# Two row blocks of a gMLP input normalized and transposed earlier, in the seam between two stages

## The chip, the cores and the metric

The kernel runs on one core of a Trainium2 chip. The metric is the device time of one execution in microseconds (us), the median of several runs. Unless another source is named, times inside the execution come from one profiled execution and are counted from the start of its span.

## The reference, cut to what matters

A transformer-like block in bf16: a recurrent attention with a small memory, then a gated MLP that also mixes over the sequence (gMLP). B is 1, S is 2048, the model width 512.

```python
h  = x + A(layernorm(x))          # A: 64 segments of 32 rows, 32 heads of 128, each segment
                                  #    attends to itself and to 8 memory rows that the segment before left
xn = layernorm(h)
z  = gelu(xn @ w_in)              # 512 -> 2 x 896
z1 = z[:, :896]
z2 = layernorm(z[:, 896:])
g  = w_sp @ z2 + b_sp[:, None]    # mixes over the 2048 rows
h2 = h + (z1 * g) @ w_out
```

`layernorm` has no scale and no offset here.

## The kernel before, in words

Everything lies in one function, `fast_path`. It writes out the instructions of every engine by hand, in program order: a small emitter appends each instruction to its engine's list, finds its dependences by named tokens, and turns them into semaphore waits. So the order in the text is the order of every engine's queue. There is no planner. (A general path for inputs that would overflow stands behind a flag and does not run.)

**Rows and row blocks.** The 2048 rows are 16 row blocks of 128 (`RB` is 16, blocks 0 to 15). `h` of a block is held in `hbuf`, two slots, block parity choosing the slot.

**First stage.** A loop over the 64 segments does the attention. Every fourth segment a block of `h` is finished by `h_done` (L691 to L697): an add on DVE (VectorE, L666), the two instructions of the layernorm's statistics on DVE (L691, L692), `1/sqrt` on POOL (GpSimd, L693 and L695), and a store of `h`. `xn2_apply` (L700, DVE) then normalizes the block into `xo`, two slots. For blocks 0 to 13 that is done inside the loop, and the block is stored to DRAM and fetched back transposed by a DMA. `z2_narrow` (L735) already computes the pre-activations of the second half of `z` for blocks 0 to 9 inside the loop, and parks them in DRAM; `z2_back` (L888) loads them again. Block 14's `h_done` is the last thing in the loop, block 15's comes after it.

**Second stage, the loop around the change (L1137 and on).** Blocks 10 to 15 are its six steps, `k` from 0 to 5:

- `z2_mm` (L1060, PE = TensorE, 8 matmuls of 128x448) and its two gelus on ACT (ScalarE, L1063) give the second half of `z` for block 10 + k.
- `z1_some(4)` (L1092, 16 matmuls of 128x512, and four gelus on ACT, L1095) does four of the 28 groups of the first half of `z`. A group covers four row blocks at once, so it needs their transposed `xn`.
- `z2_gelu` (L1123, ACT, 128x896) activates two of the parked blocks, 2k and 2k + 1.
- `z2_norm` (L1074 twice, L1076, DVE, then L1078 and L1080 on POOL) takes the layernorm statistics of a `z2` block, `z2_apply` (L1085, DVE) applies them a step later.
- `mix0` (L1099, PE, 5 matmuls of 128x512 for a `z2` block) starts the mixing over rows for five of the seven feature blocks of the first 512 columns, with the blocks that were normalized in the step before. It starts in the third step, with 15 matmuls.

In step 0, the work left over from the first stage comes between: `F_group` (L661) and `WoX_mm` (L676) on PE, four groups of `z1_some`, `WoX_scatter` (L686), then `h_done(15)`.

**Blocks 14 and 15** are not sent through DRAM. They are transposed by PE (L1159, four instructions of 128x128 for a block, from `xo` into a PSUM bank) and copied out by DVE: `xn_copy` (L1055). In the kernel before, `xn2_apply` of block 14 stands in step 1 and of block 15 in step 2; the transposes and copies of block 14 stand in step 2 and of block 15 in step 3. `z2_mm` of block 14 comes in step 4, of block 15 in step 5.

**PSUM banks.** `zbank()` hands out banks 5, 6 and 7 in turn: to each half of `z2_mm`, to each group of `z1_some` and to the transposes of a block. Each of them therefore waits until the one three takings before it has been read out, by ACT for a matmul group, by DVE's `xn_copy` for a transpose:

```python
zcnt = [0]

def zbank():
    zcnt[0] += 1
    return 5 + zcnt[0] % 3
```

**After the loop**, the last four groups of `z1`, the rest of the mixing, the gating and the output matmuls follow, bounded by PE.

**DMA loads in the seam**, all issued from the queue of SP (SyncE) in this order: `w_in1`, transposed blocks 11 to 13, parked `z2`, `wT` for the first 512 columns (L884, eight pieces of 256 KB, read by `mix0`), the transposed blocks 8, 9 and 10 (L714), the bias, `wT` for the second 512 columns, `w_out`, and `h` again.

Of the kernel before, what the change touches and what calls it, by code (L numbers as in the profile page):

```python
# [169 lines left out]
def fast_path(nc, st, keep, A_x, A_mem0, A_Wq, A_Wk, A_Wv, A_Wo, A_seg_len, B_w_in, B_w_sp, B_b_sp, B_w_out, out):  # L170
# [8 lines left out]
    RB = S // 128  # L179
    DC = D // 128  # L180
# [17 lines left out]
    def sb(name, shape, dt):  # L198
        return st.enter_context(nc.sbuf_tensor("f_" + name, shape, dt))
# [32 lines left out]
    xo = sb("xo", [128, 2, 512], BF)  # L232
    wst = sb("wst", [128, RB, 64], BF)
    ident = sb("ident", [128, 128], BF)
# [26 lines left out]
    psb = ps.bitcast(BF)  # L261
# [4 lines left out]
    def PB(b):  # L266
        return ("ps", b)

    def sp(fn, **k):
        return em.add("sp", fn, dma=True, **k)  # L270

    def pe(fn, **k):
        return em.add("pe", fn, **k)
# [4 lines left out]
    def dve(fn, **k):  # L278
        return em.add("dve", fn, **k)
# [378 lines left out]
    def F_group(rb, bank, stop=False):  # L658
        for j in range(4):
            i = (4 * rb + j) % 8  # L660
            pe(lambda e, i=i, j=j: e.matmul(ps[32 * j:32 * j + 32, bank, :], lhsT=F_sb[:, :], rhs=part[:, i, :], start=True, stop=stop,  # L661
                                            tile_position=(0, 32 * j)),
               reads=[("part", i, 0), ("part", i, 1), "F"], writes=[PB(bank)])
# [8 lines left out]
    def WoX_mm(rb, qr):  # L672
        for bg in range(8):
            b, g = bg // 4, bg % 4
            h = 16 * b + 4 * qr + g
            pe(lambda e, h=h, g=g, i=8 * qr + bg: e.matmul(ps[32 * g:32 * g + 32, WXB, :], lhsT=cTx[:, rb % 2, i, :], rhs=w_o[:, h, :],  # L676
                                                           start=(i < 4), stop=(i >= H - 4), tile_position=(0, 32 * g)),
               reads=[("cTx", rb % 2), ("Wo", h // 8)], writes=[PB(WXB)])

    def WoX_evac(rb):  # L680
        act(lambda e: e.activation(out=partx[:], in_=ps[:, WXB, :], func=ACT.Copy), reads=[PB(WXB)], writes=["partx"])

    def WoX_scatter(rb, bank, start=False):
        for c in range(4):
            q = slice(32 * c, 32 * c + 32)
            pe(lambda e, q=q, c=c: e.matmul(ps[q, bank, :], lhsT=Sc[:, q], rhs=partx[:], start=start, stop=True, tile_position=(0, 32 * c)),  # L686
               reads=["partx", "Sc"], writes=[PB(bank)])

    def h_done(rb, bank):
        F_add(rb, bank)  # L690
        dve(lambda e: e.bn_stats(out=stats[:, rb % 2, :], in_=hbuf[:, rb % 2, :]), reads=[("h", rb % 2)], writes=[("st", rb % 2)])  # L691
        dve(lambda e: e.bn_aggr(out=mv[:, rb, :], in_=stats[:, rb % 2, :]), reads=[("st", rb % 2)], writes=[("mv", rb)])  # L692
        pool(lambda e: e.tensor_scalar(out=rstd[:, rb:rb + 1], in0=mv[:, rb, 1:2], scalar1=EPS, scalar2=None, op0=ALU.add),  # L693
             reads=[("mv", rb)], writes=[("rstd", rb)])
        pool(lambda e: e.tensor_tensor(out=rstd[:, rb:rb + 1], in0=rstd[:, rb:rb + 1], in1=mhalf[:, 0:1], op=ALU.pow),  # L695
             reads=[("rstd", rb), "mhalf"], writes=[("rstd", rb)])
        sp(lambda e: e.dma_start(h_d[rb], hbuf[:, rb % 2, :]), reads=[("h", rb % 2)], writes=[("hd", rb)])  # L697

    def xn2_apply(rb, j):
        dve(lambda e: e.tensor_scalar(out=xo[:, j, :], in0=hbuf[:, rb % 2, :], scalar1=mv[:, rb, 0:1], scalar2=rstd[:, rb:rb + 1],  # L700
                                      op0=ALU.subtract, op1=ALU.mult),
            reads=[("h", rb % 2), ("mv", rb), ("rstd", rb)], writes=[("xo", j)])
# [17 lines left out]
    def xT2(rb):  # L720
        return xts[rb // 8][:, rb % 8, :, :]
# [160 lines left out]
    def load_wT(tb, after):  # L882
        for t in range(8):
            sp(lambda e, t=t: e.dma_start(wTb[tb % 2][:, t, :, :], wT_d[8 * tb + t]), reads=[("wTd", 8 * tb + t)],  # L884
               writes=[("wT", tb % 2, t)], after=after)
# [10 lines left out]
    for s in range(NSEG):  # L896
        j4 = s % 4
        rb = s // 4
# [154 lines left out]
    def xn_copy(rb, j, bank):  # L1053
        src = psb[:, bank, 0:512].rearrange("p (dc c) -> p dc c", dc=DC)
        dve(lambda e: e.tensor_copy(out=xT2(rb), in_=src), reads=[PB(bank)], writes=[("xn2T", rb)], after=[lastop["s"], lastop["x"]])  # L1055

    def z2_mm(rb, hf, bank):
        t, tok = xT2z(rb)
        for dc in range(DC):
            pe(lambda e, dc=dc: e.matmul(ps[:, bank, 0:HF], lhsT=t[:, dc, :], rhs=w_in2[:, dc, hf * HF:(hf + 1) * HF],  # L1060
                                         start=(dc == 0), stop=(dc == DC - 1)),
               reads=["w_in2", tok], writes=[PB(bank)])
        act(lambda e: e.activation(out=z2[:, rb, hf * HF:(hf + 1) * HF], in_=ps[:, bank, 0:HF], func=ACT.Gelu_apprx_tanh),  # L1063
            reads=[PB(bank)], writes=[("z2", rb, hf)], after=[lastV])
# [18 lines left out]
    def z2_apply(rb):  # L1083
        j = nslot[rb]
        dve(lambda e: e.tensor_scalar(out=z2[:, rb, :], in0=z2[:, rb, :], scalar1=mv2[:, j, 0:1], scalar2=rs2[:, j:j + 1],  # L1085
                                      op0=ALU.subtract, op1=ALU.mult),
            reads=[("z2", rb, 0), ("z2", rb, 1), ("mv2", j), ("rs2", j)], writes=[("z2", rb, 0), ("z2", rb, 1)])

    def z1_group(tb, fb, bank):
        r0 = 4 * tb  # L1090
        for dc in range(DC):
            pe(lambda e, dc=dc: e.matmul(ps[:, bank, 0:TB], lhsT=w_in1[:, dc, fb * 128:(fb + 1) * 128],  # L1092
                                         rhs=xts[r0 // 8][:, r0 % 8:r0 % 8 + 4, dc, :], start=(dc == 0), stop=(dc == DC - 1)),
               reads=["w_in1"] + [("xn2T", r) for r in range(r0, r0 + 4)], writes=[PB(bank)])
        act(lambda e: e.activation(out=z1T[:, fb, tb * TB:(tb + 1) * TB], in_=ps[:, bank, 0:TB], func=ACT.Gelu_apprx_tanh),  # L1095
            reads=[PB(bank)], writes=[("z1T", fb, tb)], after=[lastK])
# [15 lines left out]
# [3 lines that stand above are left out]
# [7 lines left out]
    def z2_gelu(rb):  # L1122
        act(lambda e: e.activation(out=z2[:, rb, :], in_=z2[:, rb, :], func=ACT.Gelu_apprx_tanh),  # L1123
            reads=[("z2", rb, 0), ("z2", rb, 1)], writes=[("z2", rb, 0), ("z2", rb, 1)])
# [6 lines left out]
    def z1_some(n):  # L1131
        for _ in range(n):
            if z1list:
                tb, fb = z1list.pop(0)
                z1_group(tb, fb, zbank())

    for k, rb in enumerate(range(NP, RB)):  # L1137
        z2_mm(rb, 0, zbank())
        if k == 0:
            F_group(RB - 1, XB)  # L1140
        z2_mm(rb, 1, zbank())
        if k == 0:
            for qr in range(4):
                WoX_mm(RB - 1, qr)
            endA = em.by_eng["pe"][-1]
            WoX_evac(RB - 1)
            load_wT(1, [endA])
            sp(lambda e: e.dma_start(w_out, B_w_out.rearrange("(fb p) d -> p fb d", p=128)), writes=["w_out"], after=[endA])
            z1_some(4)
            WoX_scatter(RB - 1, XB)  # L1150
            h_done(RB - 1, XB)
            for r in range(RB):
                sp(lambda e, r=r: e.dma_start(h_sb[:, r, :], h_d[r]), reads=[("hd", r)], writes=[("hs", r)], after=[lastQ])
        if k in (1, 2):
            xn2_apply(RB - 3 + k, k % 2)
        if k in (2, 3):
            r, j, bank = RB - 4 + k, (k - 1) % 2, zbank()
            for dc in range(DC):
                pe(lambda e, dc=dc, j=j, bank=bank: e.transpose(out=psb[:, bank, dc * 128:(dc + 1) * 128], in_=xo[:, j, dc * 128:(dc + 1) * 128],  # L1159
                                                                identity=ident[:, :]), reads=[("xo", j), "ident"], writes=[PB(bank)])  # L1160
            xn_copy(r, j, bank)
        for r in range(max(0, 2 * k - 2), min(NP, 2 * k)):
            z2_apply(r)
            mixq.append((k, r))
        z2_norm(rb)
        if k > 0:
            z2_apply(rb - 1)
            mixq.append((k, rb - 1))
            z1_some(4)
        for r in range(2 * k, min(NP, 2 * k + 2)):  # L1170
            z2_gelu(r)
            z2_norm(r)
        while mixq and mixq[0][0] < k:
            mix0(mixq.pop(0)[1])
# [28 lines left out]
    for tb in range(NTB):  # L1203
        for fb in range(len(ACC) if tb == 0 else 0, FB):
            if tb == 0:
                bank = 5 + fb % 3
            else:
                bank = gcnt % 2
# [785 lines left out]
```

## Time and profile before

| | |
|---|---|
| median of 3 runs | 886.18 us (884.33 to 886.44) |
| the profiled execution | 887.59 us, of which the span in the profile is 885.8 us |
| PE busy | 858.6 us, 97% of the span |
| DVE, ACT, POOL busy | 487.6, 457.3 and 110.6 us |
| mean granted TensorE clock | 0.994 |

The span runs from the first to the last instruction; 1.79 us of the profiled execution lie around it. PE is the TensorE matmul row, and "idle before" in a row is followed by the instruction that ended the idle time. The granted clock is a share of full speed. The loop described above lies between about 717 and 773 us.

### The profile page before, as it was taken

The page shows a single profiled execution, that of the slowest core. Times are in us where ns is not written, and L with a number is a line of the kernel's source. Part 1 is how long each engine was busy: PE and PEld are TensorE (multiplying, and loading weights), DVE is VectorE, ACT ScalarE, POOL GpSimd, SP SyncE. Part 2 cuts the span into 40 slices and gives each one's busy share as a digit, 9 for nine tenths or more (in the row PEclk, how much of TensorE's full clock was granted, in tenths as well). Part 3 has the DMA queues.
Part 4 walks back from the last instruction along what each step waited for, and adds up shares of the span by engine and source line. Part 5 has one row for each costly group of instructions (what it writes and reads, how often), then busy time and mean ns, then how long its engine had stood idle before and what let it go on. Part 6 is the DMA issues. An engine that isn't in the chain of part 4 may idle for free.

```text
span 885.8 us, 46595 instructions
## 1 busy us (share of the span) xinstructions
PE 858.6 (97%) x21446; PEld 488.5 (55%) x21453; DVE 487.6 (55%) x1128; ACT 457.3 (52%) x1147; POOL 110.6 (12%) x280
## 2 busy tenths in 40 slices
PE   6889999999999999999999999999999998999997
PEld 6645555565566655656565555555555543444443
DVE  3445556565556556565655565556555557364343
ACT  2346565666665656666665666466665575400000
POOL 1420111111111111010101011111101013200000
PEclk9999999999999999999999999999999999999999
DMA  9962232123320311211312121523222299032101
GB/s 320 377 177 63 64 57 61 44 59 63 60 58 25 84 46 32 65 45 52 60 43 52 46 66 47 102 69 78 73 62 67 62 244 333 2 101 76 62 13 38
DMA packets 109210, 76.35 MB, mean 86 GB/s; under 512 B 64104, under 2 KB 94512, under 8 KB 109008
## 3 DMA queue, kind: packets, MB, share of 16 engines
q1 hardware_dynamic: 108496, 73.04, 30.1%
q8 instruction: 170, 2.79, 1.3%
q14 instruction: 32, 0.26, 0.1%
q0 software_dynamic: 192, 0.20, 0.1%
q10 hardware_dynamic: 320, 0.07, 0.0%
HBM read 41.75 MB, written 20.91 MB: 71 GB/s over the span
## 4 chain that ended last, share of the span: by engine, by line
PE 94%; DVE 2%; issue 1%; DMA 1%; POOL 1%; ACT 0%; DVEq 0%
PE f_ps L481 26%; PE f_ps L625 13%; PE f_ps L575 12%; PE f_ps L1099 11%; PE f_ps L411 7%; PE f_ps L676 4%; PE f_ps L592 3%; PE f_ps L430 3%; PE f_ps L1188 3%; PE f_ps L1092 2%; PE f_ps L735 2%; PE f_ps L520 2%; PE f_ps L541 1%; PE f_ps L511 1%; PE f_ps L649 1%
## 5 line engine op out<-in xcount | busy, mean ns | idle before, releaser
L481 PE MATMUL f_ps<-f_arena,f_hT 128*32 128x512 bf16 x4096 | 240.3, 380 | 0.5 <-issue 0.2
L488 ACT ACTIVATE f_Tst<-f_ps 128x512 bf16<-128x512 f32 x256 | 145.9, 596 | 78.1 <-PE f_ps L481 77.9
L481 PEld LDWEIGHTS f_ps<-f_arena,f_hT 128*32 128x32 bf16 x4096 | 92.9, 96 | 104.0 <-ACT f_hT L654 32.7
L575 PE MATMUL f_ps<-f_arena,f_hT 128*32 128x512 bf16 x2048 | 140.4, 378 | 0.0
L625 PE MATMUL f_ps<-f_arena,f_cT 128*32 128x256 bf16 x4096 | 129.2, 274 | 0.9 <-ACT f_cT L611 0.8
L625 PEld LDWEIGHTS f_ps<-f_arena,f_cT 128*32 128x32 bf16 x4096 | 101.2, 97 | 21.7 <-ACT f_cT L611 18.7
L494 DVE STREAM_TRANSPOSE f_QT<-f_Tst 128x256 uint32<-128x256 uint32 x128 | 57.0, 446 | 91.7 <-ACT f_Tst L488 91.7
L1099 PE MATMUL f_ps<-f_arena 128*128 128x512 bf16 x448 | 100.9, 382 | 0.0
L613 DVE TENSOR_SCALAR f_cT<-f_ps 128x320 bf16<-128x320 f32 x128 | 56.9, 487 | 41.2 <-PE f_ps L598 41.2
L1099 PEld LDWEIGHTS f_ps<-f_arena 128*128 128x128 bf16 x448 | 44.1, 99 | 53.9 <-issue 2.2
L497 DVE STREAM_TRANSPOSE f_KT<-f_Tst 128x256 uint32<-128x256 uint32 x128 | 57.0, 445 | 29.1 <-ACT f_Tst L488 26.4
L411 PE MATMUL f_ps<-f_hTe,f_arena 128*128 128x128 bf16 x1024 | 68.0, 225 | 4.0 <-DVE f_arena L422 2.9
L611 ACT ACTIVATE f_cT<-f_ps 128x320 bf16<-128x320 f32 x128 | 49.0, 435 | 38.4 <-PE f_ps L598 38.4
L411 PEld LDWEIGHTS f_ps<-f_hTe,f_arena 128*128 128x128 bf16 x1024 | 60.3, 101 | 14.1 <-issue 9.5
L504 POOL COPY f_QT<-f_arena 128x256 bf16<-128x256 bf16 x64 | 30.7, 479 | 298.2 <-PE f_ps L526 298.1
L561 DVE SCALAR_TENSOR_TENSOR f_E_sb<-f_R_sb,f_E_sb 128x160 bf16<-128x160 f32 x128 | 41.7, 325 | 46.2 <-ACT f_R_sb L557 46.2
L642 DVE CAST f_part<-f_ps 128x256 bf16<-128x256 f32 x64 | 27.2, 425 | 68.9 <-PE f_ps L625 68.9
L553 ACT ACTIVATE f_R_sb<-f_ps 128x160 f32<-128x160 f32 x128 | 39.0, 305 | 37.9 <-PE f_ps L546 37.9
L575 PEld LDWEIGHTS f_ps<-f_arena,f_hT 128*32 128x32 bf16 x2048 | 45.2, 95 | 21.1
L1105 DVE TENSOR_TENSOR f_arena<-f_ps,f_arena 128x512 f32<-128x512 f32 x28 | 19.3, 690 | 60.7 <-PE f_ps L1099 60.7
L654 ACT ACTIVATE f_hT<-f_ps 128x16 bf16<-128x16 f32 x126 | 23.2, 184 | 55.1 <-PE f_ps L649 54.7
L633 POOL COPY f_cTx<-f_cT 128x256 bf16<-128x256 bf16 x64 | 25.6, 400 | 197.1 <-DVE f_cT L613 197.1
(113 smaller groups left out, 1165.8 us busy)
## 6 DMA issues: line engine op xcount, KB each, us to landing
wT_d<-f_wst SPq DMA_DIRECT2D x32, 256.0 KB, 2.3
f_arena<-wT_d SPq DMA_DIRECT2D x32, 256.0 KB, 5.1
f_arena<-in_A_Wq_dram SPq DMA_DIRECT2D x4, 1024.0 KB, 8.8
f_arena<-in_A_Wk_dram SPq DMA_DIRECT2D x4, 1024.0 KB, 14.2
f_arena<-in_A_Wv_dram SPq DMA_DIRECT2D x4, 1024.0 KB, 14.8
f_arena<-in_A_Wo_dram SPq DMA_DIRECT2D x4, 1024.0 KB, 13.6
f_Vx<-vext_d SPq DMA_DIRECT2D x62, 64.0 KB, 2.8
vext_d<-f_Vs SPq DMA_DIRECT2D x24, 128.0 KB, 2.0
```

Of the source, the lines that this page charges most:

```text
L411: pe(lambda e, h=h, dc=dc, hh=hh: e.matmul(ps[:, bank, hh * 128:(hh + 1) * 128], lhsT=ws[:, dc, h * DH:(h + 1) * DH], rhs=hTe[:, ck % 3, d ...
L481: pe(lambda e, dc=dc, c=c, rhs=rhs: e.matmul(ps[32 * c:32 * c + 32, bank, :], lhsT=hT[:, sl, dc, :], rhs=rhs, start=(dc == 0), stop=(dc == ...
L488: act(lambda e: e.activation(out=Tst[:, tb, :].rearrange("p (hp i r) -> p hp i r", i=32, r=2), in_=ps[:, bank, :].rearrange("p (hp r i) -> ...
L494: dve(lambda e: e.transpose(out=dst, in_=src), reads=[("T", tb)], writes=[("QT", b)])
L497: dve(lambda e: e.transpose(out=dst, in_=src), reads=[("T", tb)], writes=[("KT", b)])
L553: act(lambda e: e.activation(out=R_sb[:, b, :], in_=ps[:, bank, 224:384], func=ACT.Ln, scale=LNS), reads=[PB(bank)], writes=[("R", b)])
L561: dve(lambda e: e.scalar_tensor_tensor(out=E_sb[:, b, 0:160], in0=R_sb[:, b, :], scalar=RK, in1=E_sb[:, b, 0:160], op0=ALU.mult, op1=ALU.m ...
L575: pe(lambda e, dc=dc, c=c, c0=c0: e.matmul(ps[32 * c:32 * c + 32, bank, :], lhsT=hT[:, sl, dc, :], rhs=w_v[:, dc, c0:c0 + 512], start=(dc ...
L611: act(lambda e: e.activation(out=dst, in_=src, func=ACT.Copy, scale=UNSC), reads=[PB(PVB[c])], writes=[("cT", c)])
L613: dve(lambda e: e.tensor_scalar(out=dst, in0=src, scalar1=UNSC, scalar2=None, op0=ALU.mult), reads=[PB(PVB[c])], writes=[("cT", c)])
L625: pe(lambda e, h=h, g=g, i=i, b=b, c=c: e.matmul(ps[32 * g:32 * g + 32, bank, 0:d1 - d0], lhsT=cTh[:, i, 8:40], rhs=w_o[:, h, d0:d1], star ...
L1099: pe(lambda e: e.matmul(ps[:, bank, 0:TB], lhsT=z2[:, sc, fb * 128:(fb + 1) * 128], rhs=wTb[tb % 2][:, :, sc, :], start=(n == 0), stop=(n ...
```

## The change

`xn2_apply(14)` moves from step 1 to a place ahead of the loop, so that it stands in DVE's queue behind the last instructions of the first stage and ahead of `h_done(15)`. Block 14's transposes and its `xn_copy` move from step 2 to step 0, behind `WoX_mm` and ahead of the four `z1` groups on PE, and ahead of `h_done(15)` on DVE. `xn2_apply(15)` moves from step 2 to step 1. Block 15's transposes and copy stay in step 3. The slots of `xo` that the two blocks use are swapped. No instruction is added or removed, and no DMA and no POOL instruction changes its place. The turn of the banks shifts: from step 0 to step 2 each taker gets the next bank of the ring.

```diff
+    def xn2T_pe(rb, j):
+        bank = zbank()
+        for dc in range(DC):
+            pe(lambda e, dc=dc: e.transpose(out=psb[:, bank, dc * 128:(dc + 1) * 128], in_=xo[:, j, dc * 128:(dc + 1) * 128],
+                                            identity=ident[:, :]), reads=[("xo", j), "ident"], writes=[PB(bank)])
+        xn_copy(rb, j, bank)
+
+    xn2_apply(RB - 2, 0)
     for k, rb in enumerate(range(NP, RB)):
         z2_mm(rb, 0, zbank())
         if k == 0:
             F_group(RB - 1, XB)
         z2_mm(rb, 1, zbank())
         if k == 0:
             for qr in range(4):
                 WoX_mm(RB - 1, qr)
             endA = em.by_eng["pe"][-1]
             WoX_evac(RB - 1)
             load_wT(1, [endA])
             sp(lambda e: e.dma_start(w_out, ...), writes=["w_out"], after=[endA])
+            xn2T_pe(RB - 2, 0)
             z1_some(4)
             WoX_scatter(RB - 1, XB)
             h_done(RB - 1, XB)
             ...
-        if k in (1, 2):
-            xn2_apply(RB - 3 + k, k % 2)
-        if k in (2, 3):
-            r, j, bank = RB - 4 + k, (k - 1) % 2, zbank()
-            for dc in range(DC):
-                pe(lambda e, dc=dc, j=j, bank=bank: e.transpose(out=psb[:, bank, dc * 128:(dc + 1) * 128], in_=xo[:, j, dc * 128:(dc + 1) * 128],
-                                                                identity=ident[:, :]), reads=[("xo", j), "ident"], writes=[PB(bank)])
-            xn_copy(r, j, bank)
+        if k == 1:
+            xn2_apply(RB - 1, 1)
+        if k == 3:
+            xn2T_pe(RB - 1, 1)
         for r in range(max(0, 2 * k - 2), min(NP, 2 * k)):
             z2_apply(r)
             mixq.append((k, r))
         z2_norm(rb)
         if k > 0:
             z2_apply(rb - 1)
             mixq.append((k, rb - 1))
             z1_some(4)
         for r in range(2 * k, min(NP, 2 * k + 2)):
             z2_gelu(r)
             z2_norm(r)
         while mixq and mixq[0][0] < k:
             mix0(mixq.pop(0)[1])
```

## The prediction

> **What bounds the kernel now.** I read the page first: PE is busy for nearly all of the span, so only a wait of PE itself, or slow work on it, is worth anything, and the change touches PE's queue only in the seam between the stages. The windows of that seam come next. Their columns are the length, then busy time and instructions of PE, PEld, DVE, ACT and POOL, then the granted clock.
>
> ```profile
> core 0: us, PE busy (x) PEld busy (x) DVE busy (x) ACT busy (x) POOL busy (x), PEclk, DMA share, GB/s
> ...
> 731.98:737.48 5.50, 2.29 (x13) 0.91 (x12) 5.32 (x14) 3.02 (x6) 2.26 (x7) 1.00 1.37 247
> 737.48:744.14 6.66, 6.66 (x23) 2.69 (x24) 5.11 (x12) 2.87 (x4) 2.17 (x6) 0.74 1.03 380
> ```
>
> From 731.98 to 737.48 PE works for 2.29 us of 5.50 while DVE works for 5.32: here DVE is the bound. In the next window PE is busy but at a mean clock of 0.74. The timeline of PE shows the places; in brackets is the idle time before a row and what ended it.
>
> ```profile
> 721.44 3.63 PE L1092 MATMUL f_ps<-f_arena 128*128 128x512 bf16 x16
> ...
> 730.47 1.68 PE L1060 MATMUL f_ps<-f_arena 128*128 128x448 bf16 x8
> 731.98 0.39 PE L1159 MATMUL f_ps<-f_ident,f_xo 128*128 128x128 bf16 x4
> 733.43 1.90 PE L1092 MATMUL f_ps<-f_arena 128*128 128x512 bf16 x8 [1.06 <-ACT f_arena L1063]
> 737.48 2.36 PE L1092 MATMUL f_ps<-f_arena 128*128 128x512 bf16 x8 [2.15 <-DVE f_arena L1055]
> 739.63 4.67 PE L1099 MATMUL f_ps<-f_arena 128*128 128x512 bf16 x15
> 744.14 1.68 PE L1060 MATMUL f_ps<-f_arena 128*128 128x448 bf16 x8
> 745.66 0.39 PE L1159 MATMUL f_ps<-f_ident,f_xo 128*128 128x128 bf16 x4
> 745.88 3.62 PE L1092 MATMUL f_ps<-f_arena 128*128 128x512 bf16 x16
> 749.33 3.40 PE L1099 MATMUL f_ps<-f_arena 128*128 128x512 bf16 x15
> 752.57 1.68 PE L1060 MATMUL f_ps<-f_arena 128*128 128x448 bf16 x8
> ```
>
> From start to start, undisturbed work costs: transposes of a block 745.88 − 745.66 = 0.22; 16 z1 matmuls 749.33 − 745.88 = 3.45, so 0.863 a group; 15 mixing matmuls 752.57 − 749.33 = 3.24; a z2 block 731.98 − 730.47 = 1.51. Between 731.98 and 744.14, 12.16 us, PE does one transposition, 16 z1 and 15 mixing matmuls: 0.22 + 3.45 + 3.24 = 6.91. So 5.25 us are lost, in three pieces:
>
> - The first z1 group could start at 732.20 and starts at 733.43: 1.23, ended by the gelu of z2 block 12.
> - The third could start at 733.43 + 1.73 = 735.16 and starts at 737.48: 2.32, ended by `xn_copy(14)`, whose bank it takes.
> - Then two groups take 2.15 instead of 1.73, the mixing 4.51 instead of 3.24: 0.42 + 1.27 = 1.69, the half clock.
>
> The chain that ended last says why that copy is late:
>
> ```profile
> 725.45 0.70 DVE f_hbuf L666
> ...
> 736.81 0.28 DVE f_xo L700
> 737.09 0.34 DVE f_arena L1055
> ```
>
> From 725.45, the add of block 15, nearly all of it is DVE (and one POOL step): statistics and applications of the z2 blocks, one after the other, with the copy at the end, five microseconds after the transposes at 731.98.
>
> **The change part by part.** *Front.* Block 14's application moves ahead of the loop and its transposes and copy into step 0.
>
> ```profile
> 719.12 0.18 DVE L692 BATCH_NORM_AGGREGATE f_mv<-f_stats 128x2 f32<-128x6 f32 x1
> ```
>
> ```profile
> 719.69 0.57 POOL L695 TENSOR_TENSOR f_rstd<-f_rstd,f_mhalf 128x1 f32<-128x1 f32 x1
> ```
>
> The statistics are there at 719.30, POOL's root at 720.26; the application, 0.28 in the chain, ends by about 720.7 with a margin. PE comes to the transposes at 721.44, so they wait for nothing. They cost 0.22 on PE here and save 0.22 in step 2. DVE has nothing else to do before 725.45; the copy, 0.34, ends at about 722.2, and its bank is wanted by the third z1 group at 721.66 + 1.73 = 723.39. The new wait of `xn_copy(14)` has `h_done(15)` behind it on DVE, but that needs PE's work at 725.00 anyway. Bounds of this part: 0.22 if the next group follows as it did in step 3, 0.39, the whole row of four transposes, if nothing overlaps; no wait of PE stands there that could shrink, so no gain. I take 0.22, the measured distance. Then everything up to step 2 runs 0.22 later. The queues of SP and POOL keep their order, so nothing is moved past a DMA.
>
> *Step 2.* z2 block 12 ends at 732.20 and no transposes follow. By the shifted turn of the banks the first group no longer waits for block 12's first gelu; the second does.
>
> ```profile
> 731.16 1.78 ACT L1123 ACTIVATE f_arena<-f_arena 128x896 bf16<-128x896 bf16 x2
> 732.84 0.97 ACT L1063 ACTIVATE f_arena<-f_ps 128x448 bf16<-128x448 f32 x2
> ...
> 740.37 1.78 ACT L1123 ACTIVATE f_arena<-f_arena 128x896 bf16<-128x896 bf16 x2
> ```
>
> ```profile
> 733.79 0.46 DVE L1085 TENSOR_SCALAR f_arena<-f_arena,f_mv,f_rs 128x896 bf16<-128x896 bf16 x1
> ```
>
> ACT is held up by two 128x896 gelus until 732.94, and PE got its bank at 733.43; with the shift 733.65. So group 1 runs 732.20 to 733.06, 0.59 is lost, groups 2 to 4 run 733.65 to 736.24. The mixing needs block 10's application, which ended at 734.25, now 734.47: no wait. At full clock it runs 736.24 to 739.48, against 744.14: **4.66 us gained** here, which is 5.25 less the 0.59 that stays.
>
> *What is late next.* Block 15's copy, in step 3, still stands behind two statistics in DVE's queue.
>
> ```profile
> 737.34 1.09 DVE L1085 TENSOR_SCALAR f_arena<-f_arena,f_mv,f_rs 128x896 bf16<-128x896 bf16 x2
> ...
> 741.35 1.15 DVE L1074 BATCH_NORM_STATS2 f_st<-f_arena 128x6 f32<-128x448 bf16 x2 [1.23 <-ACT f_arena L1123]
> ...
> 743.79 0.21 DVE L1076 BATCH_NORM_AGGREGATE f_mv<-f_st 128x2 f32<-128x12 f32 x1
> ```
>
> ```profile
> 737.25 0.63 POOL L1080 TENSOR_TENSOR f_rs<-f_rs,f_mhalf 128x1 f32<-128x1 f32 x1
> ```
>
> One would think that DVE is 0.62 ahead, the application and the copy taken out (0.28 + 0.34). But the second of the two L1085 there waits for POOL's root of block 3, ready at 737.88, now 738.10: the pair still ends 0.22 later, at 738.65. DVE was free for block 4's statistics at 741.35 − 1.23 = 740.12, now 740.34. There it waited for ACT; now ACT is early (its two gelus began 0.74 after the mixing, now at 736.98, and end at 738.76). The statistics of blocks 4 and 5 took 741.35 to 744.00, so now 740.34 to 742.99, and the copy ends at 743.33; PE restarted 0.05 after the last copy. In step 3 PE does z2 block 13 (739.48 to 740.99), the transposes (to 741.21) and two groups (to 742.94), and the third group wants that bank: it waits until 743.38, **0.44 us lost**. Behind the copy DVE has lost nothing against PE: the rest of its queue stands as it stood, and PE is 4.2 earlier instead of 4.7.
>
> *Loads.* PE comes 4.7 us earlier to what SP has fetched.
>
> ```profile
> f_arena<-wT_d SPq DMA_DIRECT2D x2, 256.0 KB, 5.8
> ```
>
> ```profile
> f_arena<-xn_d SPq DMA_TRANSPOSE x2, 5.7
> ```
>
> These are the last pieces of `wT`, in flight from 729.2 to 729.85, and the last transposed blocks (732.3 to 733.7): issue plus landing gives 735.0 to 735.7 and 738.0 to 739.4 as estimates. They are wanted at 736.24 and, by the first group of blocks 8 to 11, at 742.94. Margins 0.6 and 3.5.
>
> **Sum:** 4.66 − 0.44 = 4.2 us. Between the bounds: nothing lost in step 3 and half the wait in step 2 gives 5.0; the front at 0.39 and step 3 twice as bad gives 3.6. The profiled execution would go from 887.59 to 883.4, its span with it and the 1.8 around it unchanged. It stands 1.4 above the median of 886.18, so the median goes to 882.0.
>
> **The clock.** Is the half clock owed to this wait?
>
> ```profile
> 29.06 3.45 PE L411 MATMUL f_ps<-f_hTe,f_arena 128*128 128x128 bf16 x32 [2.85 <-DVE f_arena L422]
> ...
> 52.52 1.96 PE L411 MATMUL f_ps<-f_hTe,f_arena 128*128 128x128 bf16 x32 [1.04 <-ACT f_V_sb L582]
> ```
>
> ```profile
> 30.00:31.00 1.00, 1.00 (x12) 1.00 (x11) 0.01 (x1) 0.00 (x0) 0.69 (x3) 0.50 1.04 385
> ```
>
> ```profile
> 50.00:100.00 50.00, 46.34 (x1374) 26.01 (x1378) 25.96 (x64) 27.44 (x72) 6.72 (x15) 1.00 0.31 79
> ```
>
> An idle time of 2.85 is followed by clock 0.50, one of 1.04 by none. Idle times of 1.23 and 2.32 with 1.73 of work between are nearer to the first; the 0.59 and 0.44 that stay are shorter than the second. So I count the 1.69 as gained. [...]
>
> **The rivals.** *The stall moves to step 3* (chance 0.12). For it: the copy stands in the same queue. Against it: nothing ahead of it can end more than 0.22 later than in the profile of before, 744.00 + 0.22. Then PE restarts at 744.61 instead of 742.94, a loss of 1.67: gain 3.0, 883.2. With a half clock of 1.69 after it the gain is 1.3, 884.9.
>
> *The half clock is not owed to the wait and comes all the same* (0.10). For it: the sum of the idle times is below no measured edge. Against it: the rows above. The gain is 4.2 − 1.69 = 2.5, 883.7. [...]
>
> *A load is late* (0.05): `wT` has a margin of 0.6; a piece that lands at 737.2 costs 1.0, gain 3.2, 883.0. It can't take more than the gain, since PE came later before.
>
> *Slower* (0.05): the transposes at the front make PE wait, with 16 z1 matmuls and everything else behind them. It needs block 14's application late, by POOL or by the semaphores. From 720.7 to 721.44 nothing is lost; the gain is used up when `xo` comes at 721.44 + 4.2 − 1.69 = 724.0, with a half clock of 1.69 for that gap. If it comes 5 us after that point, at 729.0, about when block 15's own application could follow its add at 725.45, the loss is 7.6 + 1.69 − 4.2 = 5.0: 891.2. Against it: POOL is idle there and DVE has nothing queued ahead.
>
> That the change does not do what it says is excluded by the written order: transposes and copy are moved in both queues.
>
> **How the numbers follow.** The forecast, 882.0, has 0.68; its own range is 881.2 to 882.6 by the bounds of the sum, and 0.8 wider below, because one of the three runs of before lies 1.8 under the median. To hold 8 in 10 the range reaches to 884.4, over the late load, the half clock and the milder half of the moved stall. A measurement tells about 0.3% from no change, 2.7 us, so faster means under 883.5: the forecast but for a small part, the late load, over half of the moved stall, 0.77; the rest of that and the half clock make 0.17 the same; 0.06 slower.
>
> **What would show it.** In the timeline of PE after: transposes at about 721.4 with no idle time before them; no row with an idle time ended by L1055 before step 3, and there one of 0.3 to 0.6; the 15 mixing matmuls beginning at about 736.2 and taking 3.2; clock 1.00 in both windows. In the list of waits, PE's wait for ACT's L1063 in step 2 stays, at 0.4 to 0.6. Wrong would be: an idle time ahead of the transposes; a wait of over 1.5 for L1055 in step 3; clock 0.5 anywhere between 730 and 760; mixing matmuls released by a DMA.

## The result

| | before | after | ratio |
|---|---|---|---|
| first comparison, median | 886.02 us (8 runs) | 880.19 us (8 runs) | 0.9957 (0.9937 to 0.9978) |
| second comparison, another session | 884.01 us (17 runs) | 880.80 us (12 runs) | 0.9963 (0.9949 to 0.9976) |
| profiled execution, span | 885.8 us | 877.6 us | |
| the seam | 31.13 us | 26.82 us | |

The ratios have 95% intervals. The second is close to the quotient of its medians, 0.9964; the first is not, since 880.19 / 886.02 is 0.9934, and why it lies higher is not known here. By these ratios the change makes the kernel faster by 0.4%, within bounds of 0.2 and 0.6%. The seam is the stretch that the change touches: from PE's first instruction behind `WoX_mm` to the start of z2 block 14 in step 4. Before it ran from 721.44 to 752.57, after from 717.45 to 744.27. The timeline of PE after:

```profile
717.45 0.40 PE L1140 MATMUL f_ps<-f_ident,f_xo 128*128 128x128 bf16 x4
717.68 3.62 PE L1092 MATMUL f_ps<-f_arena 128*128 128x512 bf16 x16
...
723.09 3.78 PE L1092 MATMUL f_ps<-f_arena 128*128 128x512 bf16 x16
726.70 1.68 PE L1060 MATMUL f_ps<-f_arena 128*128 128x448 bf16 x8
728.22 1.03 PE L1092 MATMUL f_ps<-f_arena 128*128 128x512 bf16 x4
729.66 2.76 PE L1092 MATMUL f_ps<-f_arena 128*128 128x512 bf16 x12 [0.42 <-ACT f_arena L1063]
732.26 3.40 PE L1099 MATMUL f_ps<-f_arena 128*128 128x512 bf16 x15
735.50 1.68 PE L1060 MATMUL f_ps<-f_arena 128*128 128x448 bf16 x8
737.02 0.39 PE L1140 MATMUL f_ps<-f_ident,f_xo 128*128 128x128 bf16 x4
737.24 1.89 PE L1092 MATMUL f_ps<-f_arena 128*128 128x512 bf16 x8
739.29 1.90 PE L1092 MATMUL f_ps<-f_arena 128*128 128x512 bf16 x8 [0.17 <-DVE f_arena L1055]
741.03 3.40 PE L1099 MATMUL f_ps<-f_arena 128*128 128x512 bf16 x15
744.27 1.68 PE L1060 MATMUL f_ps<-f_arena 128*128 128x448 bf16 x8
```

Block 14's transposes (L1140) stand at the front without any idle time. In step 2 the wait for the copy (L1055) is gone, and a wait of 0.42 for ACT is left; the 15 mixing matmuls take 735.50 − 732.26 = 3.24 instead of 4.51. In step 3 a wait of 0.17 for block 15's copy has appeared. The windows of the two steps show the full clock where it was 0.74 (the columns are as before):

```profile
core 0: us, PE busy (x) PEld busy (x) DVE busy (x) ACT busy (x) POOL busy (x), PEclk, DMA share, GB/s
727.00:732.30 5.30, 4.88 (x25) 2.11 (x23) 4.77 (x13) 4.72 (x8) 2.24 (x6) 1.00 1.22 283
732.30:741.00 8.70, 8.53 (x44) 3.93 (x43) 7.34 (x18) 5.15 (x8) 4.07 (x9) 1.00 1.06 375
```

And the chain that ended last still runs through DVE's queue up to a copy; it is now block 15's, a step later:

```profile
738.74 0.21 DVE f_mv L1076
738.95 0.30 DVE f_arena L1055
739.25 0.05 issue
739.29 1.90 PE f_ps L1092 x8
```

The two spans differ by 8.2 us, but the seam only by 31.13 − 26.82 = 4.31. The rest, 721.44 − 717.45 = 3.99, arose ahead of the seam, where the two kernels are the same code in the same order. The experiments show what that is worth.

### The profile page after: what moved, and what is told of

It reads as the page before. It is cut to its first block, busy times and chain, and to the rows that moved or that the text cites. A ratio compares the mean times of both kernels' runs of the same rounds, so it can differ in the third digit from the quotient of the medians.

```text
span 877.6 us, 46595 instructions
## 1 busy us (share of the span) xinstructions
PE 854.7 (97%) x21446; PEld 487.1 (56%) x21453; DVE 487.4 (56%) x1128; ACT 456.8 (52%) x1147; POOL 110.8 (13%) x280
## 4 chain that ended last, share of the span: by engine, by line
PE 94%; DVE 3%; DMA 1%; issue 1%; POOL 1%; ACT 0%; DVEq 0%
PE f_ps L481 26%; PE f_ps L625 13%; PE f_ps L575 12%; PE f_ps L1099 11%; PE f_ps L411 7%; PE f_ps L676 4%; PE f_ps L592 3%; PE f_ps L430 3%; PE f_ps L1193 3%; PE f_ps L1092 2%; PE f_ps L735 2%; PE f_ps L520 2%; PE f_ps L541 1%; PE f_ps L511 1%; DVE f_st L1074 1%; PE f_ps L649 1%
## 5 line engine op out<-in xcount | busy, mean ns | idle before, releaser
L625 PE MATMUL f_ps<-f_arena,f_cT 128*32 128x256 bf16 x4096 | 127.3, 272 | 0.8 <-ACT f_cT L611 0.8
```

What stands on the lines that cost most here:

```text
L625: pe(lambda e, h=h, g=g, i=i, b=b, c=c: e.matmul(ps[32 * g:32 * g + 32, bank, 0:d1 - d0], lhsT=cTh[:, i, 8:40], rhs=w_o[:, h, d0:d1], star ...
```

## The experiments

The theory: PE's wait in step 2 comes from the place of block 14's copy in DVE's queue, behind the statistics of the z2 blocks, through the bank that the copy holds; and a wait that is long enough costs a stretch of half clock, that is, a time in which the granted clock is 0.50. The rivals: the late application was the cause; the bank has no part in it; the clock falls for another reason.

**Only the applications early.** The changed kernel, with both transposes and copies back in steps 2 and 3:

```diff
-            xn2T_pe(RB - 2, 0)
...
-        if k == 3:
-            xn2T_pe(RB - 1, 1)
+        if k in (2, 3):
+            xn2T_pe(RB - 4 + k, k - 2)
```

> The changed kernel, but block 14's transposes and its copy go back to step 2; only the two applications (xn2_apply) stay early. Measured as the seam: from PE's first instruction behind WoX_mm to the start of z2 block 14 (31.13 us before, 26.82 after). Theory (the copy is late because it stands in DVE's queue behind the statistics of the z2 blocks): the copy comes only one application earlier, 0.28 us, the wait of PE for L1055 in step 2 is 1.8 to 2.0, the half clock stays, seam 30.7 to 30.9. If a wait of 2.0 no longer costs the half clock: 29.1. Rival (the late application was what held the copy up): no such wait, seam 26.8.

```profile
730.82 0.39 PE L1140 MATMUL f_ps<-f_ident,f_xo 128*128 128x128 bf16 x4
732.27 1.90 PE L1092 MATMUL f_ps<-f_arena 128*128 128x512 bf16 x8 [1.06 <-ACT f_arena L1063]
735.99 1.90 PE L1092 MATMUL f_ps<-f_arena 128*128 128x512 bf16 x8 [1.82 <-DVE f_arena L1055]
737.72 3.40 PE L1099 MATMUL f_ps<-f_arena 128*128 128x512 bf16 x15
```

The wait for the copy stays at 1.82, 0.33 less than the 2.15 of before. So it is the copy's place that counts, and the application's is worth 0.3: the rival falls. But the mixing matmuls run at full clock, against the theory's first figure: the seam took 749.39 − 720.28 = 29.11, the figure given for the case without half clock. Between these two executions a wait shorter by 0.33 saved 2.0 us, of which 1.69 is the half clock.

**Only another bank.** The kernel before, with block 14's transposes in a bank that no z1 group takes:

```diff
-            r, j, bank = RB - 4 + k, (k - 1) % 2, zbank()
+            r, j, bank = RB - 4 + k, (k - 1) % 2, (0 if k == 2 else zbank())
```

> The kernel before, but block 14's transposes in step 2 go to PSUM bank 0, which the mixing takes next, instead of one of the three banks in turn. No engine's order is changed. Theory (the z1 group waited for the bank that the late copy holds): the z1 groups no longer wait for L1055; the first mixing matmul, which takes bank 0, waits for it instead, 1.4 to 1.5 us, until the copy ends as late as before; with about 0.4 of wait for ACT the idle time is 1.9 instead of 3.55. Seam 27.7 if so little idle time costs no half clock, 29.4 if it does. Rival (the bank does not matter): 31.1. Rival on the clock (the half clock has nothing to do with the waits): 29.4 with the same half clock at about the same time.

```profile
731.20 1.03 PE L1092 MATMUL f_ps<-f_arena 128*128 128x512 bf16 x4
732.43 2.76 PE L1092 MATMUL f_ps<-f_arena 128*128 128x512 bf16 x12 [0.20 <-ACT f_arena L1063]
736.48 3.41 PE L1099 MATMUL f_ps<-f_arena 128*128 128x512 bf16 x15 [1.29 <-DVE f_arena L1055]
```

As expected: the z1 groups no longer wait for L1055, the first mixing matmul does, and the clock stays full. The seam is 748.15 − 720.44 = 27.71, the figure forecast for that case. The bank passes the wait on, and one edit of a bank number, with every engine's order unchanged, brings 31.13 − 27.71 = 3.42 of the 4.31; 1.69 of this is again the half clock. The edit also does a little more than its text says: since these transposes no longer take a bank of the ring, the first z1 group gets one that has long been read out, and the second the one of z2 block 12's first half, as in the changed kernel. That is why the second group and not the first waits for ACT here.

**Only block 14.**

```diff
-        if k == 1:
+        if k == 2:
             xn2_apply(RB - 1, 1)
```

> The changed kernel, but block 15's application goes back to step 2. Theory (the gain is block 14's, and DVE waits for POOL in step 2 anyway, which hides 0.28): seam 26.8 to 26.9, the wait for L1055 in step 3 at 0.1 to 0.3. Rival (block 15's earlier application is part of the gain): its 0.28 comes on top of the wait for L1055 in step 3, seam 27.1.

The seam took 748.00 − 721.20 = 26.80, and the wait in step 3 was 0.15. So block 15's earlier application brings nothing: DVE waits for POOL at that place, 0.76 us in the changed kernel and 0.46 here, and the application disappears in this wait.

These three runs are single executions. Their whole times, 885.03, 883.29 and 883.09 us against 882.88 for one execution of the kernel before taken beside them, show no gain at all. Executions differ ahead of the seam by up to 4.3 us, whichever kernel it is (shown below), which is why the seam is compared.

**A ladder of waits.** Ten waits of different lengths in the mixing of the later columns:

```diff
-    def mix(tb, fb, sc, bank, n):
+    def mix(tb, fb, sc, bank, n, after=()):      # `after` is handed on to the matmul
...
+            hold = []
+            if (tb, fb) in HOLD:                 # HOLD gives 0 to 7
+                for _ in range(HOLD[tb, fb]):
+                    dve(lambda e: e.tensor_scalar(out=xo[:, 0, :], in0=xo[:, 1, :], ...), ...)
+                hold = [em.by_eng["dve"][-1]]
             for sc in range(RB):
-                mix(tb, fb, sc, bank, sc)
+                mix(tb, fb, sc, bank, sc, hold if sc == 0 else ())
```

> The changed kernel, with ten waits of PE made on purpose in the mixing of the second to fourth 512 columns: the first matmul of a group waits for the last DVE instruction, behind which 0 to 7 extra normalizations of 128x512 (0.3 us each) are queued; they write a buffer that nothing reads. Gives idle times of PE from about 0.7 to 3.5 us, 8 to 10 us apart, each with the clock granted after it. Theory (a wait costs the half clock once it is long enough, with an edge between 1.04 and 2.3 us): idle times under some edge leave the clock at 1.00, longer ones are followed by about 3.4 us at 0.50, as in the kernel before. [...] Rival (the half clock is not tied to a wait): no relation of idle time and clock. Time 15 to 30 us over the changed kernel.

Four of the ten rows, from the timeline of PE, and the windows behind two of them; the third column from the end is the clock:

```profile
807.72 5.31 PE L1099 MATMUL f_ps<-f_arena 128*128 128x512 bf16 x16 [2.45 <-DVE f_xo L1219]
...
844.71 5.31 PE L1099 MATMUL f_ps<-f_arena 128*128 128x512 bf16 x16 [2.01 <-DVE f_xo L1219]
...
866.64 3.63 PE L1099 MATMUL f_ps<-f_arena 128*128 128x512 bf16 x16 [2.73 <-DVE f_xo L1219]
...
895.16 7.08 PE L1099 MATMUL f_ps<-f_arena 128*128 128x512 bf16 x32 [3.80 <-DVE f_xo L1219]
```

```profile
846.00:847.00 1.00, 1.00 (x3) 0.30 (x2) 0.00 (x0) 0.00 (x0) 0.00 (x0) 0.50 0.00 0
...
896.00:897.00 1.00, 1.00 (x6) 0.49 (x5) 0.00 (x0) 0.00 (x0) 0.00 (x0) 1.00 0.00 0
```

16 matmuls take 3.63 at full clock and 5.31 after a hit, which is what a wait followed by the half clock is called from here on; a wait that is not is spared. The waits of 2.01 and 2.45 were hit, those of 2.73 and 3.80 spared. So length alone does not decide, and the theory as stated fell. The starts of the four stretches of half clock, read from windows of 0.25 us, are 807.87, 831.76, 845.41 and 879.54; their distances, 23.89, 13.65 and 34.13, are 7, 4 and 10 times 3.413. That gave a new theory, worked out from these readings alone: the starts lie on a grid of 3.41 us, and a stretch follows a cell of it with 2.0 us or more of idle time. On this grid the wait of 3.80 lies across a boundary, with 1.84 and 1.96 in two cells; the 2.73 with 1.99 and 0.74; the 2.01 lies in one cell. (The run took 915.17 us, 34 more than the changed kernel and not 15 to 30: the waits came out at 1.56 to 3.80, longer than expected.)

**The same ladder again**, without any edit, to test that.

> The kernel with the ten made waits once more, not changed at all. In the first run waits of 2.01, 2.45, 2.90 and 3.35 us were followed by the half clock, waits of 1.56, 1.80, 1.84, 2.29, 2.73 and 3.80 were not, and the four stretches of half clock began whole multiples of 3.41 us apart. Theory (a grid of 3.41 us runs freely, and the clock falls at the end of a cell in which PE was idle for 2.0 us or more): the waits are the same length, the ones hit are others, and on the grid that this run shows each hit wait has at least 2.0 us in one cell and no other has; waits of 1.56 to 1.84 are never hit. Rival (the place or the length decides): the same four waits are hit again.

```profile
806.98 3.63 PE L1099 MATMUL f_ps<-f_arena 128*128 128x512 bf16 x16 [2.46 <-DVE f_xo L1219]
...
842.28 5.31 PE L1099 MATMUL f_ps<-f_arena 128*128 128x512 bf16 x16 [2.00 <-DVE f_xo L1219]
...
892.51 8.77 PE L1099 MATMUL f_ps<-f_arena 128*128 128x512 bf16 x32 [3.81 <-DVE f_xo L1219]
```

The waits have the same lengths, but others are hit: the 2.46, hit the first time, is spared, and the 3.81, spared the first time, is hit. The stretches begin at 828.86, 842.50, 876.64 and 893.71, distances of 4, 10 and 5 times 3.41. In both runs together all eight waits that were hit have 2.00 or more in one cell, and of the twelve that were spared eleven have at most 1.99. One is at odds: the 2.46, with 2.03 in its fuller cell. So the edge is about 2.0 here and not sharper than these readings, some 0.03. The rival, that the same four waits are hit again, fell.

**The kernel before again.**

> The kernel before once more, for a second profile. Theory (waits of 1.06 and 2.15 stay, and the half clock after them depends on where they fall in a grid of 3.41 us): the waits for L1063 and L1055 in step 2 are 1.0 to 1.1 and 2.1 to 2.2 again; the seam is 31.1 with the half clock or 29.4 without it, and the half clock comes only if the 2.15 has at least 2.0 in one cell of the grid. The start of the seam (721.4 in the first profile) moves by up to some us either way, without any difference of the code. Rival (the half clock belongs to this place): 31.1 again.

```profile
732.17 1.90 PE L1092 MATMUL f_ps<-f_arena 128*128 128x512 bf16 x8 [1.06 <-ACT f_arena L1063]
736.22 2.46 PE L1092 MATMUL f_ps<-f_arena 128*128 128x512 bf16 x8 [2.15 <-DVE f_arena L1055]
738.48 4.57 PE L1099 MATMUL f_ps<-f_arena 128*128 128x512 bf16 x15
```

The same two waits to 0.01, and the half clock again, from 737.42; the cell that ends there holds all of the 2.15. In the first profile the cell ending at 738.78 held 2.11 of it. The seam is 751.31 − 720.19 = 31.12. That is also what the rival foretold, so this run does not decide between the two; the ladder does. Two profiles with the half clock do not tell how often it comes; that stays an estimate: 2.15 has 2.0 in one cell unless a boundary falls into its inner 1.85, which, with the boundary taken as equally likely anywhere, leaves 1.56 of 3.41, under half of the executions. A stretch in every execution of the kernel before would lower the mean granted clock of a run by 0.0019 (half of 3.41 in 883 us). The means of the second comparison are 0.9967 over 17 runs before and 0.9970 over 12 after, which speaks against every execution, but single runs scatter by 0.001 and the share stays open.

**The changed kernel again.**

> The changed kernel once more, against the kernel before in five rounds. The seam should be 26.8 again, with a wait for ACT of about 0.4 in step 2 and one of 0.1 to 0.3 for L1055 in step 3. Theory (the seam is all of the gain: 4.3 us when the half clock comes in the kernel before, 2.6 when not): the times differ by 2.6 to 4.3 us, ratio 0.995 to 0.997. Rival (the change also gains in the attention stage, as the first pair of profiles might suggest, where the changed kernel entered the seam 4.0 us earlier): 6 to 8 us, ratio 0.991 to 0.993.

The seam is 747.22 − 720.40 = 26.82 once more, with waits of 0.42 and 0.16; the ratio was 0.9963 (0.9949 to 0.9976), within the theory's bounds, and the rival's 0.991 to 0.993 lies outside. This execution entered the seam at 720.40 and not at 717.45. Part of the difference is one row of PE in the attention stage:

```profile
562.44 2.55 PE L481 MATMUL f_ps<-f_arena,f_hT 128*32 128x512 bf16 x43 [1.41 <-issue]
```

In the first profile of the changed kernel this idle time is missing. Most of the 3.99 between the first two profiles arose at about the same place: from the add (L666) of one row block to the next, 549.44 to 573.37 before and 548.79 to 569.69 after, the kernel before took 23.93 and the changed one 20.90, 3.03 less. The windows there, before and after, show that the kernel before lost clock there too, in a stretch of half clock from 557.87:

```profile
550.00:575.00 25.00, 23.16 (x632) 12.86 (x628) 12.97 (x34) 12.74 (x35) 3.33 (x8) 0.93 0.52 100
```

```profile
550.00:575.00 25.00, 24.17 (x740) 13.04 (x732) 14.85 (x38) 15.45 (x40) 3.82 (x9) 1.00 0.47 111
```

Its second profile had none there. In the eight profiles without made waits, the seam begins between 717.10 and 721.44, whichever kernel it is. So the 3.99 is not the change's. What the "issue" waits are was not settled.

**The change carried on.** The second long gelu of a step goes behind the next step's two z2 gelus:

```diff
+    later = []
...
         z2_mm(rb, 1, zbank())
+        if k == 3:
+            xn2T_pe(RB - 1, 1)
+        for r in later:
+            z2_gelu(r)
+            z2_norm(r)
+        later = []
...
-        if k == 3:
-            xn2T_pe(RB - 1, 1)
...
-        for r in range(2 * k, min(NP, 2 * k + 2)):
+        for r in range(2 * k, min(NP, 2 * k + 1)):
             z2_gelu(r)
             z2_norm(r)
+        later = list(range(2 * k + 1, min(NP, 2 * k + 2)))
```

> The changed kernel, carried on against the two waits that are left in it: of the two gelus of parked blocks (128x896) that end a step on ACT, the second moves behind the next step's two z2 gelus, and with it its statistics on DVE, and block 15's transposes and copy come ahead of those statistics in step 3. The order within PE and DVE is otherwise the same. Theory (PE waits in steps 1 and 2 for z2's gelu because it stands behind two long gelus, and in step 3 for a copy behind two statistics): the losses left in the changed kernel's profile, 0.16 in step 1, 0.59 in step 2 and 0.34 in step 3, go; seam 25.7 to 25.9 against 26.82, time 0.9 to 1.1 us less than the changed kernel. Rival (the first z1 group's own gelu becomes late behind the moved gelu, so that the fourth group waits): seam 26.2 to 26.6. Rival (wT lands late for the earlier mixing): an idle time ahead of the 15 mixing matmuls, released by a DMA.

```profile
727.70 3.62 PE L1092 MATMUL f_ps<-f_arena 128*128 128x512 bf16 x16
731.16 3.40 PE L1099 MATMUL f_ps<-f_arena 128*128 128x512 bf16 x15
734.39 1.68 PE L1060 MATMUL f_ps<-f_arena 128*128 128x448 bf16 x8
735.91 0.39 PE L1140 MATMUL f_ps<-f_ident,f_xo 128*128 128x128 bf16 x4
736.13 3.62 PE L1092 MATMUL f_ps<-f_arena 128*128 128x512 bf16 x16
```

No idle time is left in any step, and neither rival's wait appears. The seam is 742.82 − 717.10 = 25.72, 1.10 less than in the changed kernel. The median is 879.02 against 884.01 of the kernel before, ratio 0.9949 (0.9929 to 0.9969), the fastest of the three; against the changed kernel's 880.80 in the same session, 1.8 less, no interval was taken.

## Why the prediction was right

It forecast 882.0 from 886.18, a ratio of 0.9953; measured were 0.9957 and 0.9963. The first median itself, 880.19, lies 5.8 below its partner, more than the seam gives.

- *The seam.* Forecast 4.66 − 0.44 = 4.22, measured 4.31. Taking off the 3.99 by which this profile is early, the mixing was forecast at 732.25 and began at 732.26.
- *Front.* No wait, 717.68 − 717.45 = 0.23 for the transposes: 0.22 was right. The slower rival did not occur.
- *Step 2.* The wait for ACT moved to the second group and stayed: 732.26 − 728.22 less 3.45 gives 0.59, as forecast.
- *Step 3.* The stall that was said to come next came, smaller: 741.03 − 737.24 less 3.45 is 0.34, not 0.44, and the idle time in the row is 0.17, under the 0.3 to 0.6 that had been named as its sign. The copy ended at 739.25, which is 743.24 in the times of before and 0.09 earlier than forecast. That DVE gains nothing in step 2, because POOL's root is waited for there, is shown by the run with block 14 alone.
- *Loads.* No row of PE in the seam is released by a DMA in the two profiles of the changed kernel; the last piece of `wT` landed 1.7 and 1.85 us ahead of the mixing. But in the second run of the ladder, whose seam is that of the changed kernel, PE waits 0.38 ahead of the 15 mixing matmuls. The row names DVE's L1074, yet the last piece of `wT` landed only at 734.50, and the mixing began at 734.60. That seam took 746.26 − 719.24 = 27.02. So the rival of the late load is real, with a small price: 0.2 in one of four executions.
- *The clock.* The 1.69 was rightly tied to the wait, and the rival that it comes all the same fell. But the reason, a length nearer to 2.85 than to 1.04, was incomplete: in the ladder a wait of 2.00 was hit and one of 3.80 was spared, and the idle time in the fuller cell of 3.41 us sorts all but one of the twenty waits. The 1.69 is saved only in those executions in which the kernel before loses it; both of its profiles did, and how many others do was not shown. The forecast, made against an execution with the half clock, was an upper case; without it the seam would give 4.31 − 1.69 = 2.6. The measured ratios, worth 3.3 to 3.8 us, lie between the two. By the estimate above, a stretch in 1.56 of 3.41 executions, the mean gain would be 2.6 + 0.8 = 3.4. That the time came so near to 882.0 is thus in part luck: the profiled execution happened to have the half clock, and the sum counted it in full.
- *Outside the sum.* The forecast left the time ahead of the seam unchanged. Single executions differ there by up to 4.3 us, as much as the whole gain, so one pair of spans (8.2 apart) says little about this change. The seam repeats to 0.01 in two profiles of the kernel before and in three executions of the changed one, and to 0.2 in the fourth, with the late load.

## What to carry to other kernels

When PE waits for a copy, look at what stands ahead of that copy in its engine's queue, and at whose bank it holds: in this seam the place in the queue was worth 4.3 us and the bank alone 3.4, each with the 1.7 of a half clock that both profiles of the kernel before show and that, by the estimate above, does not come in every execution; normalizing earlier was worth only the 0.3 by which it shortened the queue, and that clock. Compare a local change by its own stretch between two fixed instructions, since the rest of the span may wander by more. Between the matmuls of 512 columns, eight waits of PE of 2.00 to 3.81 us in the two ladder runs cost up to another 1.7 us in half clock, while six others of 2.29 to 3.80 and all six of 1.56 to 1.84 did not; in step 2, with a wait for the copy of 1.82 instead of 2.15, the seam was 2.0 us shorter, six times what the wait lost. And check the name that a profile gives to a wait against the landing of the loads that the instruction also needs.

## What the runs showed of the hardware

The stretches of half clock that were read began whole multiples of 3.41 us apart within their execution: at 28.80, 557.87 (in the attention stage) and 738.78 in the first profile of the kernel before, 155 and 53 times 3.413; at 29.87 and 876.37 in the first profile of the changed kernel, 248 times; and in the two ladder runs 7, 4 and 10 times and 4, 10 and 5 times. But for the one at 876.37, which the end of the span at 877.6 cuts, they lasted about 3.4 us, as from 28.80 to 32.22. The grid is a reading of these starts, and its place against the program was not the same in both ladder runs: the wait of 2.45 lay whole in one cell the first time, and the second time, as 2.46, with 0.43 and 2.03 in two. In the matmuls of 512 columns of the second stage, a cell with about 2.0 us of idle time (hit at 2.00, spared at 1.99 and once at 2.03) was followed by a stretch of half clock. In the ladder it cost 1.7 us of work in six cases of eight (5.31 instead of 3.63, 8.77 instead of 7.08); where part of the stretch passed in idle time it cost 1.6 and 1.4 (5.25 and 5.01). The wait of 3.80, with 1.84 and 1.96 in two cells, was spared; the 3.81 of the second run, with 1.59 and 2.22, was hit.

This edge does not carry over to the attention stage, with its many smaller matmuls. There the stretch from 557.87 in the first profile of the kernel before follows a cell (554.46 to 557.87) in which PE was busy for 2.01 us, so idle for only 1.40. A cell with 1.24 of idle time (49.28 to 52.69) in the same profile was spared, and one with 1.26 (50.35 to 53.77) in the first profile of the changed kernel. In the run with block 14 alone, PE was idle for 1.96 in one piece, up to 563.25, with the clock at 1.00 from 550 to 575; where the cells lie in that run is not shown. What decides there is open.
